# Cosine attention and a gelu MLP: a new order of the opening and the second batch, and scalings shared by two engines

## The chip, the cores and the metric

The kernel runs on one core of a Trainium2 chip. The metric is device time in microseconds of one execution, as the median of several runs; less is better. One further execution, recorded by the hardware profiler, gives the trace that all stage times come from.

## The reference

The computation is attention with normalised queries and keys, followed by a two-layer MLP with the exact gelu. In short:

```python
# q, k, v: [8, 12, 448, 64] float32, tau = 0.1
q_n = q / (norm(q, axis=-1) + 1e-6)
k_n = k / (norm(k, axis=-1) + 1e-6)
attn = softmax((q_n @ k_n.T) / tau)
o = attn @ v
x = o.transpose(0, 2, 1, 3).reshape(3584, 768)   # heads side by side
h = x @ w_in                                     # 768 x 2048
y = gelu_exact(h) @ w_out                        # 2048 x 768, float32
```

## The kernel before, in words

**Tiling.** Four heads of a batch are a *quad*: three quads per batch, 24 in all, numbered 0 to 23. A quad's sequence of 448 is cut into 7 chunks of 64 rows per head. The very first quad is worked in two halves of two heads, so the kernel counts *units*: units 0 and 1 are the halves of quad 0, unit 2 is quad 1, unit 3 is quad 2, and so on. Tiles of loaded data carry the quad's number (`qk0`, `sq0_0` for the squares of Q, `sq0_1` for those of K, `qkb0` for the scaled bf16 copy, `qkT0` for its transpose); the tiles around a norm (`nq`, `rn`) carry the number of a *group* of units whose roots are taken together.

**The steps of a quad.** `load_qk` (L127) loads Q and K with DMAs that SyncE issues (the first K by ScalarE), into a pool of four buffers. `square` (L173 on ScalarE, L175 on another engine) squares them, `reduce` (L183, VectorE) sums over the 64 elements of a row. `logs` and `roots` (ScalarE, L190 and L195) take the square root as exp(0.5 ln), into a tile `root2` or `root4` that has the 1e-6 beside each root; `inverses` (L201 and L203, VectorE) adds it and takes the reciprocal `rn`. `scale` (L219) multiplies Q and K with `rn` and writes bf16: 448 columns for a half of quad 0, 896 for Q or K of a whole quad. `transposes` turns the result, either on TensorE (L236, into a PSUM tile `tp` that `copies`, L241, brings back to SBUF on VectorE) or by a DMA (L231, issued by SyncE). `scores` (L257) multiplies K and Q of two chunks into one pair of PSUM banks, `exps` (L267, ScalarE) takes the exponential into bf16. The row sums come from `sums` (TensorE) or from folded additions of VectorE (`gather`) or GpSimd, `turned`, `inverted` and `spread` (VectorE) make their reciprocals, `values` (L346, TensorE) multiplies with v, and `normalise` (L380, VectorE) writes the batch's `x_t`, bf16.

**The MLP.** For one batch `mm` (L493, called the *hp* passes) accumulates 16 tiles of 128 columns of w_in over six slices of 128 rows (`kd`), 96 passes per batch; `gelu` (L522, L1357) evicts each. Two batches share one `g`. The second matmul (L427, the *op* passes) runs in *pieces* of 16 passes (one per `kf`, four small matmuls each); the last pass of a piece evicts it with a VectorE reduction (L436), or with a ScalarE copy and a VectorE addition (L434) where the caller asks for that. `run(n)` issues the next n passes from the list that `output_pieces` makes. Batch 0 has six pieces in that list, of three tiles by two halves of the columns.

**What sets the order.** Nothing schedules automatically: each engine executes its instructions in the order in which the Python code issues them, and waits by semaphores for what others have to deliver. For the first three batches this order is written out by hand in `opening()` (L538), a list of some 500 calls in which the attention of quads 0 to 2, the hp passes of batch 0, the attention of quads 3 to 5 with op passes between, and the start of batch 1's MLP are interleaved. Later batches follow rules in `attention` and `first`.

**Queues.** SyncE issues the loads of q and k, the transposing DMAs and the stores, in order. GpSimd issues the loads of v, of w_in (`load_wi`, L467: parts 0 and 1 hold kd 0 to 3 for all columns, parts 2 and 3 hold kd 4 and 5 for half of the columns each; two DMAs a part) and of w_out (`load_wo`, L473, four parts), all between its arithmetic. `late_copy` (L1371) is a copy of one column on GpSimd that waits for quad 0's last data; it stands ahead of GpSimd's first load. `spin` (L489) issues matmuls whose result nobody uses. `behind` and `rest_v` hold back the rest of batch 1's v until an exponential is done.

Of the kernel before, what the change touches and what calls it, by code (L numbers as in the profile page):

```python
# [16 lines left out]
def kernel(  # L17
# [17 lines left out]
    nc = tc.nc  # L35
# [444 lines left out]
    def upto(f, n, last=None):  # L480
        last = {load_qk: NG, load_v: NV, root: len(groups), load_wi: NQ + 1, load_wo: 4}.get(f, NU)
# [56 lines left out]
    def opening():  # L538
        load_qk(0)
        table(EXP_SET)  # L540
        load_qk(1)
        load_qk(2)
        spin(20)
        late_copy()
        load_qk(3)
        x_t[0] = xp.tile([128, KD, S], BF16, tag="x", name="x0")
        square(0, ((AC, Q),))
        square(0, ((AC, K),))
        reduce(0, Q)
# [44 lines left out]
        spin(2)
        scores(0, ((0, 4), (0, 5)))
        scale(2, ((GP, 0),))
        reduce(3, Q)
        exps(0, ((0, 4), (0, 5)))
        spin(1)
        scores(0, ((1, 0), (1, 1)))  # L600
        reduce(3, K)
        exps(0, ((1, 0), (1, 1)))
        spin(1)
        scores(0, ((1, 2), (1, 3)))
        scale(2, ((GP, 1),))
        load_qk(5)
        transposes(2, 0)
        exps(0, ((1, 2), (1, 3)))
        sums(0, (0,))
        copies(2, 0)  # L610
        scores(0, ((1, 4), (1, 5)))
        logs(3)
        scores(0, ((0, 6), (1, 6)))
        roots(3)
        transposes(2, 1)
        exps(0, ((1, 4), (1, 5)))
        inverses(3)
        sums(0, (1,))
        scale(3, ((GP, 0),))
        copies(2, 1)  # L620
        sums(0, (2,))
        exps(0, ((0, 6), (1, 6)))
        sums(0, (3,))
        sums(0, (4,))
        scores(1, ((0, 0), (1, 0)))
        scores(1, ((0, 1), (1, 1)))
        sums(0, (5,))
        exps(1, ((0, 0), (1, 0)))
        sums(0, (6,))
# [24 lines left out]
        exps(1, ((0, 4), (1, 4)))
        sums(1, (1,))
        scores(1, ((0, 5), (1, 5)))
        normalise(0, 0)
        transposes(3, 1)
        exps(1, ((0, 5), (1, 5)))
        scores(1, ((0, 6), (1, 6)))  # L660
        copies(3, 1)
        sums(1, (2,))
        square(4, ((GP, Q),))
        square(5, ((GP, Q),))
        square(5, ((GP, K),))
        load_wo(0)
        load_wo(1)
        exps(1, ((0, 6), (1, 6)))
# [767 lines left out]
```

## Time and profile before

| | us |
|---|---|
| median of three runs | 391.37 (391.14 to 391.41) |
| span of the profiled execution | 390.6 |
| TensorE busy in it | 382.6 (98%) |
| VectorE busy | 273.0 (70%) |
| ScalarE busy | 269.9 (69%) |
| GpSimd busy | 248.7 (64%) |
| mean granted TensorE clock | 1.000 of full speed |

The span runs from the first to the last instruction of the profiled execution; the runs' time of that execution is not recorded, and the median of the runs lies 0.8 above the span. Engines are PE (TensorE matmuls), PEld (its weight loads), DVE (VectorE), ACT (ScalarE), POOL (GpSimd) and SP (SyncE). In rows of groups stand the line and engine, the operation, the tile written and the tiles read, the count, and then busy time, mean nanoseconds of one and the idle time before with what ended most of it. In rows of a timeline stand the start, the length, the engine and the operation. A row of busy times by stretch has the stretch, its length, then the busy microseconds and counts of PE, PEld, DVE, ACT and POOL, the granted clock, the DMA share and the rate in GB/s. Line numbers are those of the kernel before.

### The profile page before, as it was taken

Reading aid. Unit: us, or ns where it says so; the run is one execution under the profiler, and the core shown is the slowest. Engines: PE = TensorE matmul, PEld = TensorE weight load, DVE = VectorE, ACT = ScalarE, POOL = GpSimd, SP = SyncE. Lnnn points to the kernel's source line nnn. Section 1 sums busy time; section 2 is a strip of 40 time slices with the busy share of each in tenths; the row PEclk is TensorE's granted clock in tenths of the full one; section 3 lists DMA queues with packets and bytes.
Section 4 is the critical chain, followed back from the end, with each engine's and each line's share of the span. In section 5 each row is a group of like instructions: output and inputs, shape, how many; then the busy total and the mean of one; then the engine's idle time right before and its main releaser. Section 6 shows DMA issues by size and latency. Waiting matters only on the chain.

```text
span 390.6 us, 13166 instructions
## 1 busy us (share of the span) xinstructions
PE 382.6 (98%) x5820; PEld 236.6 (61%) x5820; DVE 273.0 (70%) x509; ACT 269.9 (69%) x391; POOL 248.7 (64%) x161
## 2 busy tenths in 40 slices
PE   7899999999999999999999999999999999999996
PEld 3444568555777656865567556775567555655674
DVE  4878439876778896879696896889685993670032
ACT  5895789857999958996678767997577646504300
POOL 4796950557998399969594794969595770910000
PEclk9999999999999999999999999999999999999999
DMA  8999999926899691889067490876045600130033
GB/s 265 264 262 229 176 191 329 254 56 157 179 203 299 112 217 69 185 158 275 5 172 130 120 243 2 185 131 118 3 91 81 154 9 2 44 82 2 7 79 83
DMA packets 64473, 54.85 MB, mean 140 GB/s; under 512 B 38688, under 2 KB 60320, under 8 KB 64416
## 3 DMA queue, kind: packets, MB, share of 16 engines
q1 hardware_dynamic: 54464, 41.79, 42.0%
q0 software_dynamic: 9568, 11.80, 18.5%
q8 instruction: 45, 0.74, 0.8%
q10 hardware_dynamic: 384, 0.43, 0.4%
q14 instruction: 12, 0.10, 0.1%
HBM read 45.61 MB, written 11.01 MB: 145 GB/s over the span
## 4 chain that ended last, share of the span: by engine, by line
PE 95%; DMA 2%; SPq 1%; ACT 1%; issue 0%; DVE 0%; ACTq 0%
PE hp L493 37%; PE op L427 36%; PE st L257 9%; PE o L346 8%; DMA qk<-in_k_dram 2%; PE op L451 1%; PE sm L323 1%; PE sm L332 1%; PE tp L236 1%; SPq L134 1%; ACT sq L173 0%; ACT pt L267 0%; PE spin L489 0%; DVE last L454 0%; ACT root L195 0%
## 5 line engine op out<-in xcount | busy, mean ns | idle before, releaser
L427 PE MATMUL op<-wo,g 64*64 64x384 bf16 x3456 | 167.1, 323 | 0.2 <-issue 0.2
L267 ACT ACTIVATE pt<-st 128x896 bf16<-128x896 f32 x168 | 147.2, 918 | 19.6 <-PE st L257 17.5
L493 PE MATMUL hp<-x,wi 128*128 128x448 bf16 x768 | 147.0, 353 | 0.0
L427 PEld LDWEIGHTS <-g 64*64 64x64 bf16 x3456 | 106.2, 107 | 40.9 <-issue 4.2
L493 PEld LDWEIGHTS <-wi 128*128 128x128 bf16 x768 | 74.3, 98 | 71.6 <-issue 3.2
L219 POOL TENSOR_TENSOR qkb<-qk,rn 128x896 bf16<-128x896 f32 (+1 forms) x49 | 80.4, 1662 | 46.0 <-DVE rn L203 37.9
L278 POOL TENSOR_TENSOR acc<-acc,pt 128x896 f32<-128x896 f32 x55 | 103.8, 1888 | 4.3
L436 DVE TENSOR_REDUCE ot<-op 128x384 f32<-128x768 f32 x50 | 47.3, 946 | 54.7 <-PE op L427 47.5
L1357 ACT ACTIVATE g<-hp 128x448 bf16<-128x448 f32 x96 | 46.2, 547 | 55.1 <-PE hp L493 55.1
L257 PE MATMUL st<-qkT 64*64 64x448 bf16 x672 | 62.8, 352 | 0.5 <-ACT pt L267 0.5
L183 DVE TENSOR_REDUCE nq<-sq 128x14 f32<-128x896 f32 (+1 forms) x50 | 50.4, 1036 | 13.6 <-ACT sq L173 7.1
L380 DVE TENSOR_TENSOR x<-o,rs 128x448 bf16<-128x448 f32 x48 | 27.6, 611 | 22.9 <-PE o L346 21.9
L175 POOL TENSOR_TENSOR sq<-qk 128x896 f32<-128x896 f32 x16 | 26.6, 1685 | 23.8 <-DMA qk<-in_q_dram 13.3
L346 PE MATMUL o<-pt,v 64*64 64x448 bf16 x672 | 39.5, 349 | 0.0
L290 DVE TENSOR_TENSOR acc<-acc,pt 128x896 f32<-128x896 f32 x30 | 33.0, 1099 | 1.0
L173 ACT ACTIVATE sq<-qk 128x896 f32<-128x896 f32 (+1 forms) x33 | 28.8, 901 | 4.4 <-DMA qk<-in_q_dram 3.2
L257 PEld LDWEIGHTS <-qkT 64*64 64x64 bf16 x672 | 23.1, 106 | 11.7 <-issue 3.7
L375 DVE STREAM_TRANSPOSE rs<-rc 128x448 f32<-128x448 f32 x48 | 28.1, 621 | 0.4
L278 POOL TENSOR_TENSOR acc<-pt 128x896 f32<-128x896 bf16 x11 | 20.7, 1878 | 10.9 <-ACT pt L267 10.9
L346 PEld LDWEIGHTS <-v 64*64 64x64 bf16 x672 | 21.1, 107 | 9.2 <-issue 0.2
L522 ACT ACTIVATE g<-hp 128x448 bf16<-128x448 f32 x32 | 15.4, 547 | 12.8 <-PE hp L493 12.7
L295 DVE TRANSPOSE_TENSOR_REDUCE sa<-acc 128x28 f32<-128x896 f32 x17 | 18.8, 1104 | 0.2
(54 smaller groups left out, 176.0 us busy)
## 6 DMA issues: line engine op xcount, KB each, us to landing
qk<-in_q_dram SPq DMA_DIRECT2D x23, 448.0 KB, 4.9
qk<-in_k_dram SPq DMA_DIRECT2D x23, 448.0 KB, 5.8
out_dram<-ot SPq DMA_DIRECT2D x48, 192.0 KB, 4.0
v<-in_v_dram POOLq DMA_DIRECT2D x6, 672.0 KB, 7.2
wo<-in_moe_w_out_dram POOLq DMA_DIRECT2D x4, 768.0 KB, 10.6
wi<-in_moe_w_in_dram POOLq DMA_DIRECT2D x4, 512.0 KB, 13.8
out_dram<-ot SPq DMA_DIRECT2D x12, 96.0 KB, 2.1
wi<-in_moe_w_in_dram POOLq DMA_DIRECT2D x4, 256.0 KB, 14.1
```

What stands on the lines that cost most here:

```text
L173: eng.activation(sq, t, AF.Square)
L183: nc.vector.tensor_reduce(nq_t[n][:, j, i], sq_t[g, i][:, s0:s1], mybir.AxisListType.X, ALU.add)
L219: eng.tensor_tensor(qkb[:, i, :, s0:s1].rearrange("p c s d -> p s c d"), t[:, i, s0:s1], rn[:, i].to_broadcast([128, s1 - s0, C, D]), ALU. ...
L257: nc.tensor.matmul(st[cols, n, :S], lhsT=qkT[rows, 1, c, cols], rhs=qkT[rows, 0, :, cols], start=True, stop=True, tile_position=(64 * s, 6 ...
L267: nc.scalar.activation(pt, st[:, :, :S], AF.Exp, scale=inv_tau)
L278: nc.gpsimd.tensor_tensor(acc_t[g], all_t[g][:, 0] if c == 1 else acc_t[g], all_t[g][:, c], ALU.add)
L290: nc.vector.tensor_tensor(acc_t[g], acc_t[g], all_t[g][:, c], ALU.add)
L346: nc.tensor.matmul(bank_t[g, h][cols, :S], lhsT=v_t[g][rows, s, c, :], rhs=pt_t[g, s, c][rows], start=(c == 0), stop=(c == C - 1), tile_po ...
L427: nc.tensor.matmul(ps[cols, r, :NH], lhsT=g_t[sb][rows, kf, t * 128 + 64 * c:t * 128 + 64 * (c + 1)], rhs=wo[rows, kf, ni * NH:(ni + 1) * NH],
L436: nc.vector.tensor_reduce(part, ps[:, :, :NH].rearrange("p r d -> p d r"), mybir.AxisListType.X, ALU.add)
L493: nc.tensor.matmul(t, lhsT=wi[:, kd, m * 128:(m + 1) * 128], rhs=x_t[b][:, kd, :], start=(kd == 0), stop=(kd == KD - 1))
L1357: nc.scalar.activation(g_t[sb][:, m, hf * S:(hf + 1) * S], hps.pop(m), AF.Gelu)
```

## The change

- **A new order in `opening()`.** Nearly all of its calls stand in another place. Unit 1's squares, reduces and roots are interleaved with unit 0's as before, but VectorE's copies of quad 0's transposes now precede quad 1's reduces, and on ScalarE the first exponentials precede the squares of quad 2. Both `load_v` of the first batch stand ahead of `load_wi(0)`. In the second batch the scores and exponentials of quads 3, 5 and 4 are interleaved with op passes in another sequence, with quad 5's first scores ahead of quad 4's.
- **Scalings and squares shared.** VectorE takes the scalings of K for quad 0's first half, of Q for quad 1, of K for quad 2, and of Q and K for quads 4 and 5; GpSimd had them all, and keeps the rest. GpSimd takes the square of Q for quad 0's second half and that of K for quad 2, which ScalarE had.
- **Buffers of the loads.** `gate(3)` allocates quad 3's tile early and lets GpSimd set two elements of each partition to zero in it; quad 3's load writes the same tile and so stands behind that. `late_copy`, which reads quad 0's tile, is moved into the second batch, so that this buffer stays in use until then; quads 4 and 5 take the buffers of quads 1 and 2, where they took those of quads 0 and 1.
- **Own root for quad 5.** Group 5 now holds quad 4 alone, and quad 5 is a new group 19 (`NR`) with its own tile `root6`; its logs and roots are called beside group 5's.
- **Output pieces of batch 0.** The first two pieces are interleaved: 12 passes of the first, 12 of the second, then the last 4 of each.
- `spin`: 20 + 8 passes become 20 + 2. `attend(g, c, p)` is written as its two calls in the later batches, which changes nothing there.

```diff
+    root2 += [consts.tile([128, 4 * C, 2], F32, name=f"root6_{n}") for n in range(1)]
...
+    groups[NQ + 2] = [NQ + 2]
+    NR = len(groups)
+    groups.append([NQ + 3])
...
-        t = qkp.tile([128, 2, 2, C, D], F32, tag="qk", name=f"qk{g}")
+        t = qk_t[g] if g in qk_t else qkp.tile([128, 2, 2, C, D], F32, tag="qk", name=f"qk{g}")
...
+    def gate(g):
+        qk_t[g] = qkp.tile([128, 2, 2, C, D], F32, tag="qk", name=f"qk{g}")
+        nc.gpsimd.memset(qk_t[g][:, :, 0, 0, 0:1], 0.0)
...
-        sr_t[n] = root2[2 if len(groups[n]) == 2 else n % 2][:, :math.prod(shapes[n])]
+        sr_t[n] = root2[3 if n == NR else 2 if len(groups[n]) == 2 else n % 2][:, :math.prod(shapes[n])]
...
     def opening():
...
+        scale(0, ((GP, Q),))
...
+        scale(0, ((DV, K),))
...
-        fill = [f for t, ni in todo if t not in tail for f in second_pieces(sb, t, ni)]
+        pieces = [second_pieces(sb, t, ni) for t, ni in todo if t not in tail]
+        if b == 0:
+            n = KF * 3 // 4
+            one, two = pieces[:2]
+            pieces[:2] = [one[:n] + two[:n] + one[n:] + two[n:]]
+        fill = [f for p in pieces for f in p]

Three places show how instructions move. The first is GpSimd's opening, from its first work on quad 0 to the scalings of quad 1. In the kernel before (`qkb` is the scaled copy, `rn0` and `rn1` are the reciprocals of quad 0's halves, `v0` and `v1` the loads of v, `wi` those of w_in):

```order
L1371 COPY late_166<-qk0_133 128x1
L155 DMA v0_180<-in_v_dram 128x2x448
L467 DMA wi_131<-in_moe_w_in_dram 64x2x2048 x2
L219 TENSOR_TENSOR qkb0_197<-qk0_133,rn0_192 128x7x64 x2
L219 TENSOR_TENSOR qkb0_197<-qk0_133,rn1_221 128x7x64 x2
L155 DMA v1_260<-in_v_dram 128x4x448
L467 DMA wi_131<-in_moe_w_in_dram 64x2x2048 x2
L219 TENSOR_TENSOR qkb1_297<-qk1_139,rn2_285 128x2x7x64 x2
L219 TENSOR_TENSOR qkb2_364<-qk2_142,rn3_360 128x2x7x64
```

And in the changed kernel, from the same point:

```order
L183 TENSOR_TENSOR sq0_0_141<-qk0_135 128x448
L145 MEMSET qk3_155 128x2
L163 DMA v1_157<-in_v_dram 128x4x448
L227 TENSOR_TENSOR qkb0_165<-qk0_135,rn0_163 128x7x64
L163 DMA v0_230<-in_v_dram 128x2x448
L227 TENSOR_TENSOR qkb0_165<-qk0_135,rn1_209 128x7x64 x2
L475 DMA wi_133<-in_moe_w_in_dram 64x2x2048 x2
L183 TENSOR_TENSOR sq2_1_287<-qk2_227 128x896
L227 TENSOR_TENSOR qkb1_307<-qk1_151,rn2_302 128x2x7x64
```

One scaling with `rn0` instead of two is left on GpSimd, `v1` is loaded ahead of `v0` and of that scaling, and the first `wi` loads have moved from ahead of quad 0's scalings to behind them. A square stands at the start and another ahead of quad 1's scaling, of which GpSimd keeps one half.

The second place is VectorE's opening, from the reduces of quad 0's first half. Before (`nq` are the sums of squares, `se` and `rn` the inverses, `tp` the PSUM tiles of the transposes, `qkT0` quad 0's transposed copy):

```order
L183 TENSOR_REDUCE nq0_176<-sq0_0_172 128x7
L183 TENSOR_REDUCE nq0_176<-sq0_1_174 128x7
L183 TENSOR_REDUCE nq1_184<-sq0_0_172 128x7
L201 TENSOR_REDUCE se0_190<-root2_0_125 128x14
L203 RECIPROCAL rn0_192<-se0_190 128x14
L183 TENSOR_REDUCE nq1_184<-sq0_1_174 128x7
L183 TENSOR_REDUCE nq2_201<-sq1_0_194 128x14
L201 TENSOR_REDUCE se1_219<-root2_1_126 128x14
L203 RECIPROCAL rn1_221<-se1_219 128x14
L241 COPY qkT0_208<-tp0_1_209 64x896
L241 COPY qkT0_208<-tp0_0_225 64x896
```

And changed:

```order
L191 TENSOR_REDUCE nq0_143<-sq0_0_141 128x7
L191 TENSOR_REDUCE nq0_143<-sq0_1_145 128x7
L191 TENSOR_REDUCE nq1_159<-sq0_0_141 128x7
L209 TENSOR_REDUCE se0_161<-root2_0_125 128x14
L211 RECIPROCAL rn0_163<-se0_161 128x14
L191 TENSOR_REDUCE nq1_159<-sq0_1_145 128x7
L227 TENSOR_TENSOR qkb0_165<-qk0_135,rn0_163 128x7x64
L209 TENSOR_REDUCE se1_207<-root2_1_126 128x14
L211 RECIPROCAL rn1_209<-se1_207 128x14
L249 COPY qkT0_198<-tp0_0_199 64x896
L249 COPY qkT0_198<-tp0_1_212 64x896
L191 TENSOR_REDUCE nq2_234<-sq1_0_174 128x14
```

VectorE now scales one part of `qkb0` itself, right behind the reduce of the second half, and the first two copies to `qkT0` stand ahead of the reduces of quad 1 (`nq2`), of which one stood ahead of them.

The third place is GpSimd's work behind quad 2's scaling (`qkb2`), where the last parts of w_in are loaded. Before:

```order
L219 TENSOR_TENSOR qkb2_364<-qk2_142,rn3_360 128x2x7x64
L467 DMA wi_131<-in_moe_w_in_dram 64x2x1024 x2
L219 TENSOR_TENSOR qkb2_364<-qk2_142,rn3_360 128x2x7x64
L467 DMA wi_131<-in_moe_w_in_dram 64x2x1024 x2
L175 TENSOR_TENSOR sq3_1_464<-qk3_168 128x896
L175 TENSOR_TENSOR sq3_0_492<-qk3_168 128x896
L175 TENSOR_TENSOR sq4_0_494<-qk4_241 128x896
```

And changed:

```order
L227 TENSOR_TENSOR qkb2_365<-qk2_227,rn3_363 128x2x7x64
L183 TENSOR_TENSOR sq3_1_430<-qk3_155 128x896
L475 DMA wi_133<-in_moe_w_in_dram 64x2x1024 x2
L183 TENSOR_TENSOR sq3_0_439<-qk3_155 128x896
L183 TENSOR_TENSOR sq4_0_449<-qk4_275 128x896
L475 DMA wi_133<-in_moe_w_in_dram 64x2x1024 x2
L481 DMA wo_134<-in_moe_w_out_dram 128x4x768 x2
```

The square of quad 4's Q (`sq4_0`) has moved from behind the last `wi` loads and quad 3's squares to ahead of the last `wi` loads; one of the two scalings of quad 2 is no longer here (VectorE has it).

More of the change, by code (lines that the diff above doesn't have):

```diff
@@ L612, in opening @@
-        logs(3)
-        scores(0, ((0, 6), (1, 6)))
+        exps(0, ((0, 0), (0, 1)))
+        square(3, ((GP, K),))
+        scores(0, ((0, 4), (0, 5)))
+        exps(0, ((0, 4), (0, 5)))
+        scores(0, ((1, 0), (1, 1)))
+        inverses(2)
+        exps(0, ((1, 0), (1, 1)))
+        reduce(3, Q)
+        scale(2, ((GP, K),))
+        scores(0, ((1, 2), (1, 3)))
+        exps(0, ((1, 2), (1, 3)))
+        more(0)
+        reduce(3, K)
+        scores(0, ((0, 6), (1, 6)))
+        transposes(2, 1)
@@ L663, in opening @@
[L663 to L668, printed above, removed]
+        bank(0, 13)
+        load_wo(2)
+        sums(1, (0,))
+        sums(1, (1,))
+        exps(1, ((0, 4), (1, 4)))
+        sums(1, (2,))
+        spread(0, 0)
+        copies(3, 0)
+        normalise(0, 0)
+        scores(2, ((0, 0), (1, 0)))
+        values(1, (0,))
+        values(1, (1,))
+        scores(2, ((0, 2), (1, 2)))
@@ L803, in opening @@
+        mm(0, 9, 0, 6)
+        gelu(0, 7)
+        gelu(0, 14)
+        run(1)
+        run(1)
+        run(1)
+        gelu(0, 6)
+        run(1)
+        run(1)
+        run(1)
+        run(1)
+        run(1)
+        inverses(5)
+        inverses(19)
+        copies(4, 1)
+        scale(6, ((DV, K),))
+        gelu(0, 9)
+        scores(3, ((0, 0), (1, 0)), 0)
         run(1)
@@ L805, in opening @@
         run(1)
-        gelu(0, 9)
-        scale(5, ((GP, Q),))
+        run(1)
+        scale(6, ((DV, Q),))
+        run(1)
+        run(1)
+        table(EXP_SET)
+        exps(3, ((0, 0), (1, 0)))
+        scores(3, ((0, 1), (1, 1)), 1)
+        run(1)
+        exps(3, ((0, 1), (1, 1)))
+        scale(5, ((DV, K),))
+        scale(5, ((DV, Q),))
+        behind(3, 1)
+        late_copy()
+        load_v(2)
+        rest_v()
+        run(1)
+        scores(3, ((0, 4), (1, 4)), 0)
+        exps(3, ((0, 4), (1, 4)))
@@ L808, in opening @@
+        run(1)
+        run(1)
+        run(1)
+        run(1)
+        run(1)
+        run(1)
+        run(1)
+        run(1)
+        transposes(6)
+        scores(3, ((0, 3), (1, 3)), 1)
+        run(1)
+        gather(3, 1)
+        scores(3, ((0, 2), (1, 2)), 0)
+        exps(3, ((0, 3), (1, 3)))
+        exps(3, ((0, 2), (1, 2)))
         transposes(5)
         run(1)
-        gelu(0, 13)
-        table(EXP_SET)
-        run(3)
-        scores(3, ((0, 0), (1, 0)), 0)
-        scores(3, ((0, 1), (1, 1)), 1)
@@ L833, in opening @@
+        run(1)
+        run(1)
+        run(1)
+        run(1, AC)
+        scores(5, ((0, 1), (1, 1)), 1)
+        scores(5, ((0, 6), (1, 6)), 0)
+        exps(5, ((0, 1), (1, 1)))
         gather(3, 2)
         gather(3, 3)
-        run(5)
-        attend(3, 4, 0)
+        gather(3, 4)
+        run(1)
+        run(1)
+        run(1)
+        run(1)
+        run(1)
+        run(1)
+        run(1)
+        run(1)
+        load_qk(9)
+        banks(1, 4, 3)
+        load_qk(7)
+        load_qk(6)
@@ new lines, in opening @@
+        load_qk(8)
+        exps(5, ((0, 6), (1, 6)))
+        scores(4, ((0, 6), (1, 6)), 1)
+        run(1)
+        run(1)
+        run(1)
+        square(7, ((GP, Q),))
+        square(8, ((GP, Q),))
+        scores(5, ((0, 2), (1, 2)), 0)
+        square(7, ((GP, K),))
+        square(9, ((GP, Q),))
+        square(8, ((GP, K),))
+        square(9, ((GP, K),))
+        run(1)
+        run(1)
+        run(1)
+        exps(4, ((0, 6), (1, 6)))
+        run(1)
+        load_v(3)
+        exps(5, ((0, 2), (1, 2)))
```

538 lines of the change are left out of this document (251 added, 287 removed).

## The prediction

> **What bounds the kernel now.** I read the page first, then busy times by stage, then the chain of waits in order of time, then the timelines of the opening. The page's busy row and the row of the chain that ended last:
>
> ```profile
> PE 382.6 (98%) x5820; PEld 236.6 (61%) x5820; DVE 273.0 (70%) x509; ACT 269.9 (69%) x391; POOL 248.7 (64%) x161
> PE 95%; DMA 2%; SPq 1%; ACT 1%; issue 0%; DVE 0%; ACTq 0%
> ```
>
> TensorE is busy 382.6 of 390.6 us and holds 95% of the chain. The change adds and removes no matmul except six spins (28 before, 22 after), so it can only move TensorE's idle time. Busy time by stage (columns: stretch, its length, then each engine's busy us; PEclk is the granted clock):
>
> ```profile
> 8.00:14.00 6.00, 4.37 (x41) 2.26 (x41) 4.04 (x8) 4.46 (x9) 4.86 (x6) 1.00 1.12 321
> 14.00:20.00 6.00, 5.48 (x52) 2.33 (x51) 4.92 (x9) 5.97 (x10) 4.60 (x5) 1.00 1.06 248
> 20.00:33.30 13.30, 13.29 (x189) 6.19 (x190) 10.63 (x18) 12.12 (x15) 13.28 (x12) 1.00 1.10 257
> 33.30:52.00 18.70, 18.70 (x116) 9.93 (x116) 8.64 (x16) 12.01 (x22) 15.54 (x11) 1.00 1.09 194
> 52.00:77.70 25.70, 25.70 (x586) 17.85 (x585) 20.16 (x39) 22.26 (x29) 7.71 (x6) 1.00 1.12 265
> ```
>
> A busy TensorE is not TensorE at work: between 14 and 20 us it is 5.48 busy with 52 matmuls of small tiles, three of them spins. There ScalarE is the full engine, 5.97 of 6.00. From 33.3 us on TensorE is full and useful. Three rows of the chain mark the borders:
>
> ```profile
> 3.70 8.88 DMA qk<-in_k_dram
> 12.66 0.95 ACT sq L173
> 33.35 13.35 PE hp L493 x70
> ```
>
> Up to 33.35 us TensorE waits for the first batch's attention; what comes after is work that no reordering shortens. So the gain is how much earlier than 33.35 the hp run starts, less every wait that the new order adds behind it. Any TensorE wait behind that point costs its full length.
>
> **The opening, step by step.** VectorE, GpSimd and TensorE around quad 0's first half (start, us, engine):
>
> ```profile
> 7.14 0.24 DVE L203 RECIPROCAL rn<-se 128x14 f32<-128x14 f32 x1
> 7.38 0.62 DVE L183 TENSOR_REDUCE nq<-sq 128x7 f32<-128x448 f32 x1
> 10.70 1.08 DVE L241 COPY qkT<-tp 64x896 bf16<-64x896 bf16 x2
> 5.77 0.89 POOL L155 DMA_DIRECT2D v<-in_v_dram  x1
> 6.65 1.22 POOL L467 DMA_DIRECT2D wi<-in_moe_w_in_dram  x2
> 7.86 1.86 POOL L219 TENSOR_TENSOR qkb<-qk,rn 128x448 bf16<-128x448 f32 x2
> 12.36 0.57 PE L257 MATMUL st<-qkT 64*64 64x448 bf16 x4
> ```
>
> The prices of the moved operations:
>
> ```profile
> L219 POOL TENSOR_TENSOR qkb<-qk,rn 128x448 bf16<-128x448 f32 x4 | 3.7, 951 | 1.1 <-DVE rn L203 1.1
> L219 DVE TENSOR_TENSOR qkb<-qk,rn 128x896 bf16<-128x896 f32 x1 | 1.1, 1092 | 0.0
> ```
>
> The reciprocal rn ends at 7.38. Now GpSimd is still issuing v and wi until 7.86, then scales K and Q one after the other until 9.72. After, GpSimd issues only v ahead of it and scales Q from about 7.45 to 8.4; VectorE scales K behind its reduce that ends at 8.00. That is 0.6 (half of 1.09, rounded up), or until 9.0 if it must wait for GpSimd (below). I take 9.0. The K transposes then end near 9.6, the second inverse (0.4) runs meanwhile, the two copies (1.08) end near 10.45, and the first scores start at 10.5 instead of 12.36. The old copies stood behind a reduce of quad 1 on VectorE; that reduce now stands behind them.
>
> GpSimd also takes a square of 448 (0.95 at most, by its scaling row) and one of 896 that ScalarE did. ScalarE is where the time then goes:
>
> ```profile
> 13.99 4.13 ACT L267 ACTIVATE pt<-st 128x896 bf16<-128x896 f32 x5
> 20.35 10.29 ACT L267 ACTIVATE pt<-st 128x896 bf16<-128x896 f32 x12 [0.16 <-PE st L257]
> 27.20 5.21 ACT L267 ACTIVATE pt<-st 128x896 bf16<-128x896 f32 x6
> 12.66 0.95 ACT L173 ACTIVATE sq<-qk 128x896 f32<-128x896 f32 x1 [0.97 <-DMA qk<-in_k_dram]
> ```
>
> Now the first exp starts at 13.99, because the squares of three quads come first and wait for their data (0.97 in the last row), and the 21st ends at 32.41 (27.20 + 5.21). After: exp 1 from 11.1 to 12.0; a square (0.95), a log and a root (0.55, with overlap) to 13.3; four exps at 0.80 (13.99 and 4.13 for five) to 16.5; log, exp, root, exp to 18.6; a wait of 0.3 for quad 1's copies; 14 exps at 0.86 (10.29 / 12) from 18.9 to 30.9. That is 1.5 earlier. The tail from the 21st exp to the hp run was 0.94 (33.35 - 32.41) and stays, so the hp run starts near 31.8: **gain 1.55**. With exps at 0.80 throughout it is 2.4; with the K scaling, the copies and the waits each 0.4 worse it is 0.4.
>
> The six spins removed cost nothing: the granted clock is 1.00 in every row above, also where TensorE is busy 4.37 of 6, and TensorE's longest pause in the new order is about a microsecond.
>
> **GpSimd beside VectorE.** One place shows both engines scaling at once:
>
> ```profile
> 87.84 1.09 DVE L219 TENSOR_TENSOR qkb<-qk,rn 128x896 bf16<-128x896 f32 x1
> 90.33 1.10 DVE L175 TENSOR_TENSOR sq<-qk 128x896 f32<-128x896 f32 x1
> 87.89 6.74 POOL L219 TENSOR_TENSOR qkb<-qk,rn 128x896 bf16<-128x896 f32 x3 [0.38 <-DVE rn L203]
> 14.84 3.33 POOL L219 TENSOR_TENSOR qkb<-qk,rn 128x896 bf16<-128x896 f32 x2 [0.19 <-DVE rn L203]
> ```
>
> Undisturbed, GpSimd needs 3.33 for two (1.67 each). Beside two VectorE operations on two SBUF inputs, three take 6.74 instead of 5.0, while VectorE keeps 1.09 and 1.10. So GpSimd lost 1.7 us, nearly all of the overlap, where VectorE started first by 0.05. In the new order quad 2's scaling is such a pair: the K half follows its own reciprocal on VectorE, so it should start first, near 18.9 by the sequence above, and GpSimd's Q half ends near 21.7 instead of 20.6. Its transposes on TensorE come near 21.8, after the copies of K: price about 0. The Trainium skill, "SBUF — State Buffer", section "SBUF: two separate sides", says that the pair of ports is an exclusive lock, taken by whichever starts first for its whole instruction. These rows agree for VectorE first; none shows GpSimd first, where by that rule VectorE would wait.
>
> **Loads.** Now q3 is issued at once, and q4 and q5 as soon as quads 0 and 1 have been scaled. After, q3 waits for GpSimd's memset (about 6.2), q4 for both scalings of quad 1 (about 17.2) and q5 for those of quad 2 (about 21). The wi loads start later, 11.4 instead of 6.65, behind both v loads. Traffic per queue at 19 to 23 us (v under way), then at 25 to 29 (wi); then the issue of the last wi pair, the landing times of all wi loads, and those of q4 and q5:
>
> ```profile
> q0 software_dynamic: 424, 0.38, 57.2%
> q1 hardware_dynamic: 422, 0.72, 55.6%
> q0 software_dynamic: 182, 0.68, 83.8%
> q1 hardware_dynamic: 181, 0.30, 23.1%
> 23.91 1.26 POOL L467 DMA_DIRECT2D wi<-in_moe_w_in_dram  x2
> DMA to landing us min/median/max: 10.0/14.1/17.3
> qk<-in_q_dram SPq DMA_DIRECT2D x1, 448.0 KB, 10.9
> qk<-in_q_dram SPq DMA_DIRECT2D x1, 448.0 KB, 15.9
> ```
>
> The two queues send packet for packet (424 to 422, 182 to 181), so q0 moves 0.095 MB/us of v and 0.17 of wi whatever q1 has. From about 10 us: both v (0.69 MB) to 17.3, wi's first 2.1 MB to 29.6, the last 1.05 MB to about 36.5: last landing near 37.5, like now (23.9 and 14.1 make 38.0 for the pair). The last wi piece is needed 38 hp passes into the run, at 0.190 each (row below): 31.8 + 7.2 = 39.0. Cover: 1.5 us, against 2 now. If the cover goes, TensorE waits for the difference.
>
> **Second batch.** Quads 4 and 5 are now scaled on VectorE, behind the second PE transpose of quad 3, and their transposing DMAs are used sooner (quad 5's scores come before quad 4's). For the two now, and for 96 hp and 96 op passes:
>
> ```profile
> L231 SPq DMA_TRANSPOSE qkT<-qkb x2: 2170/2468/2767, 51.9 to 54.2; - x2
> DMA to landing us min/median/max: 5.5/5.9/6.3
> 77.76 18.27 PE hp L493 x96
> 365.89 15.72 PE op L427 x384
> ```
>
> From that PE transpose: 0.5, copy 0.6, two scalings 2.2, landing 5.5 to 6.3: 8.8 to 9.6. TensorE gets there after 0.5 + 12 hp passes (2.3) + 32 op passes of 0.164 (5.2) + 5 scores of 0.19 (1.0) = 9.0. So quad 5 is late by 0 to 0.6. Quad 4's follows two scalings later (11.0 to 11.8), needed at 10.6: late by 0.4 to 1.2, the first delay included. I take 0.4, the end for the least traffic, since wo is nearly loaded then. The rest here (evictions first in the interleaved pieces, exps between) keeps covers of 0.1 to 0.5 by the same counting; I take 0 and keep 0.5 as the bound. The own root for quad 5 and the extra table load lie under the hp run, where ScalarE is 12.01 busy of 18.70. The two long pieces of tail and all later batches are untouched.
>
> **The sum.** 390.6 - 1.55 + 0.4 = 389.45 for the span, a gain of 1.15. The median of the runs, 391.37, stands 0.8 above the profiled span; I keep that: 390.2.
>
> **Rivals.**
> 1. *Given back in the second batch* (0.18): transposes at their late end (1.2) and a late eviction or exp (0.5) eat the gain: 391.5. For it: TensorE is full there, so every wait counts. Against: traffic is lower than where the 6.3 landing was seen.
> 2. *GpSimd first on the shared ports* (0.10): at quad 2, VectorE's K scaling waits out GpSimd's 1.67; TensorE's transposes, copies and ScalarE's exps shift by about 1.2, and 391.4 results. Against: in both pairs of the rows VectorE started first. This is what the skill's lock would make of the pair.
> 3. *The last wi load behind quad 4* (0.14, slower): in GpSimd's row a square on q4 now stands ahead of the last wi loads. If q4, issued at 17.2, lands after 10.9 to 15.9 like q4 and q5 now, it is there at 28.1 to 33.1, wi is issued 1.7 to 2.3 later, and with the shortest landing of its rows, 10.0, comes at 40 to 45 instead of 37.5. From 41 on (39.0 + 1.15 + 0.8) the kernel is slower; at 43 TensorE waits 4: 394.2. Against: q1 is shorter then, so q4 should land near 26.
>
> **How the numbers follow.** The measurement tells 0.2% (0.8 us) from no change. The forecast, 389.1 to 390.6, has 0.58 and is faster by more than that; rivals 1 and 2 lie within it (0.28); rival 3 is slower (0.14). The low end is a gain of 2.4 with nothing given back: 389.0. The upper end takes in rivals 1 and 2 and a wi load one microsecond late beyond its cover and the gain: 392.1.
>
> **What would show it.** In the profile after: first scores near 10.5, first exp near 11.1, 21st exp ending near 30.9, the hp run starting near 31.8, no TensorE idle until 56; wi landing before 39; quad 5's first scores with at most half a microsecond of wait. A hp run that starts after 32.6, or waits of over 1 us behind it, would make the forecast wrong.

## The result, and the profile after

| | before | after |
|---|---|---|
| median of the runs | 391.38 (14 runs, 390.36 to 393.22) | 393.64 (14 runs, 392.21 to 396.39) |
| profiled execution: span | 390.6 | 391.6 |
| hp run of batch 0 starts | 33.29 | 32.41 |
| first op pass | 51.95 | 51.17 |
| hp run of batch 1 starts | 77.69 | 78.02 |
| first op pass behind it | 95.95 | 97.01 |

The changed kernel is slower: ratio 1.0054, 95% interval 1.0037 to 1.0071. A gain of 1.2 was forecast; the time lies 2.3 above the kernel before, and above the upper end of 392.1. Each run also has a mean granted TensorE clock, and it matters here: 7 of the 14 runs of the changed kernel lie below 0.998, and below I call the others *full-clock runs* (median 392.44) and compare like with like.

The page of the changed kernel, its busy row and the chain that ended last:

```profile
PE 382.6 (98%) x5814; PEld 236.1 (60%) x5814; DVE 279.8 (71%) x519; ACT 270.9 (69%) x393; POOL 240.6 (61%) x157
PE 83%; DMA 5%; issue 4%; POOL 3%; DVE 2%; ACT 1%; SPq 1%; POOLq 0%
```

TensorE is as busy as before, but the chain now leaves it for 17% of the span instead of 5%: loads of q, squares and VectorE's work stand in it. Busy times in the stretches that were shown of before:

```profile
14.00:20.00 6.00, 5.51 (x46) 2.18 (x45) 5.42 (x8) 4.40 (x8) 3.62 (x4) 0.72 1.13 214
52.00:77.70 25.70, 24.97 (x568) 18.35 (x560) 20.95 (x39) 21.63 (x27) 7.63 (x7) 1.00 0.91 239
```

Two things are new. From 14 to 20 us the granted clock is 0.72, where it was 1.00, and ScalarE, which was full there, is busy 4.40 of 6. And between 52 and 77.7 us TensorE, which had been full, lacks 0.73. Microsecond by microsecond the clock drop looks like this (columns as before, the clock is the third number from the end):

```profile
15.00:16.00 1.00, 0.81 (x11) 0.50 (x10) 1.00 (x2) 1.00 (x3) 1.00 (x2) 1.00 1.23 223
16.00:17.00 1.00, 1.00 (x9) 0.42 (x8) 0.97 (x2) 1.00 (x4) 0.65 (x2) 0.62 1.11 225
17.00:18.00 1.00, 1.00 (x11) 0.61 (x10) 0.60 (x2) 0.89 (x2) 0.00 (x0) 0.50 1.05 209
19.00:20.00 1.00, 1.00 (x12) 0.23 (x10) 0.92 (x1) 0.52 (x1) 0.97 (x1) 0.67 1.03 209
```

The opening, in the timelines of TensorE and ScalarE:

```profile
9.89 0.56 PE L265 MATMUL st<-qkT 64*64 64x448 bf16 x4 [0.79 <-DVE qkT L249]
10.50 0.92 ACT L275 ACTIVATE pt<-st 128x896 bf16<-128x896 f32 x1 [0.64 <-PE st L265]
19.48 11.15 ACT L275 ACTIVATE pt<-st 128x896 bf16<-128x896 f32 x13 [1.60 <-PE st L265]
32.41 8.97 PE L501 MATMUL hp<-x,wi 128*128 128x448 bf16 x46
```

The first scores and the first exponential come even earlier than forecast (10.5 and 11.1), but under the half clock ScalarE waits 1.60 for scores, and of the 1.93 that e10 below has at full clock only 0.88 is left when the hp run starts. Behind it, up to 110 us, TensorE's timeline shows three waits:

```profile
71.52 0.84 PE L435 MATMUL op<-wo,g 64*64 64x384 bf16 x16 [0.59 <-DVE x L388]
82.55 14.54 PE L501 MATMUL hp<-x,wi 128*128 128x448 bf16 x76 [0.57 <-DVE x L388]
104.10 1.17 PE L435 MATMUL op<-wo,g 64*64 64x384 bf16 x24 [0.54 <-DVE ot L444]
```

From the first op pass to the next hp run the kernel before takes 25.74, the changed one 26.85; the hp run itself takes 0.73 more from its first to its last pass (18.71 against 17.98); from there to the hp run of the third batch it takes 0.24 more (34.47 against 34.23). With 0.78 gained up to the first op pass, 1.11 + 0.73 + 0.24 - 0.78 makes 1.3 lost, and what follows gives 0.2 back: the spans differ by 1.1. (Every run's time is 1.8 above its span, so that the profiled execution of before, 390.6, was a run of about 392.4 and not one at the median; the forecast's 0.8 was wrong by this.)

### The profile page after: what moved, and what is told of

It is laid out like the page before. It is cut to its first block, busy times and chain, and to the rows that moved or that the text cites. A ratio compares the mean times of both kernels' runs of the same rounds, so it can differ in the third digit from the quotient of the medians.

```text
span 391.6 us, 13173 instructions
## 1 busy us (share of the span) xinstructions
PE 382.6 (98%) x5814; PEld 236.1 (60%) x5814; DVE 279.8 (71%) x519; ACT 270.9 (69%) x393; POOL 240.6 (61%) x157
## 4 chain that ended last, share of the span: by engine, by line
PE 83%; DMA 5%; issue 4%; POOL 3%; DVE 2%; ACT 1%; SPq 1%; POOLq 0%
PE hp L501 33%; PE op L435 31%; PE st L265 8%; PE o L354 7%; DMA qk<-in_q_dram 5%; POOL sq L183 2%; PE op L459 1%; PE sm L331 1%; ACT pt L275 1%; PE tp L244 1%; SPq L138 1%; SPq L239 1%; DVE nq L191 1%; POOL qkb L227 1%; PE sm L340 0%
## 5 line engine op out<-in xcount | busy, mean ns | idle before, releaser
L435 PE MATMUL op<-wo,g 64*64 64x384 bf16 x3456 | 165.9, 323 | 1.1 <-DVE x L388 0.6
L275 ACT ACTIVATE pt<-st 128x896 bf16<-128x896 f32 x168 | 147.1, 919 | 20.8 <-PE st L265 18.8
L501 PE MATMUL hp<-x,wi 128*128 128x448 bf16 x768 | 147.5, 353 | 0.6 <-DVE x L388 0.6
L435 PEld LDWEIGHTS <-g 64*64 64x64 bf16 x3456 | 105.5, 107 | 41.3 <-issue 3.8
L501 PEld LDWEIGHTS <-wi 128*128 128x128 bf16 x768 | 74.2, 98 | 72.3 <-issue 4.2
L227 POOL TENSOR_TENSOR qkb<-qk,rn 128x896 bf16<-128x896 f32 (+1 forms) x42 | 69.7, 1677 | 48.7 <-DVE rn L211 41.8
L444 DVE TENSOR_REDUCE ot<-op 128x384 f32<-128x768 f32 x50 | 47.2, 945 | 47.7 <-PE op L435 47.6
L265 PE MATMUL st<-qkT 64*64 64x448 bf16 x672 | 63.4, 355 | 1.5 <-DVE qkT L249 0.8
L191 DVE TENSOR_REDUCE nq<-sq 128x14 f32<-128x896 f32 (+1 forms) x50 | 50.4, 1036 | 11.5 <-POOL sq L183 6.2
L183 POOL TENSOR_TENSOR sq<-qk 128x896 f32<-128x896 f32 (+1 forms) x18 | 29.3, 1640 | 29.4 <-DMA qk<-in_q_dram 20.5
L388 DVE TENSOR_TENSOR x<-o,rs 128x448 bf16<-128x448 f32 x48 | 27.6, 611 | 22.9 <-PE o L354 22.4
L265 PEld LDWEIGHTS <-qkT 64*64 64x64 bf16 x672 | 22.8, 107 | 14.0 <-issue 4.3
L181 ACT ACTIVATE sq<-qk 128x896 f32<-128x896 f32 (+1 forms) x31 | 27.3, 910 | 1.9 <-DMA qk<-in_q_dram 1.7
L530 ACT ACTIVATE g<-hp 128x448 bf16<-128x448 f32 x32 | 15.6, 544 | 12.5 <-PE hp L501 12.4
```

The source lines that it names most:

```text
L183: eng.tensor_tensor(sq, t, t, ALU.mult)
L191: nc.vector.tensor_reduce(nq_t[n][:, j, i], sq_t[g, i][:, s0:s1], mybir.AxisListType.X, ALU.add)
L227: eng.tensor_tensor(qkb[:, i, :, s0:s1].rearrange("p c s d -> p s c d"), t[:, i, s0:s1], rn[:, i].to_broadcast([128, s1 - s0, C, D]), ALU. ...
L265: nc.tensor.matmul(st[cols, n, :S], lhsT=qkT[rows, 1, c, cols], rhs=qkT[rows, 0, :, cols], start=True, stop=True, tile_position=(64 * s, 6 ...
L275: nc.scalar.activation(pt, st[:, :, :S], AF.Exp, scale=inv_tau)
L435: nc.tensor.matmul(ps[cols, r, :NH], lhsT=g_t[sb][rows, kf, t * 128 + 64 * c:t * 128 + 64 * (c + 1)], rhs=wo[rows, kf, ni * NH:(ni + 1) * NH],
```

## The experiments

Each kernel ran up to twelve times, beside runs of the kernel before on the same chip. *Full* counts runs with a mean clock of 0.998 or more, and gives their median; *stretch* is the time from the first op pass to the next hp run in the profiled execution, *run* from there to that run's last pass.

| kernel | median | full | before, full, same chip | stretch | run |
|---|---|---|---|---|---|
| e1 more spins | 393.29 | 7 of 7: 393.29 | 391.30 | 26.86 | 18.71 |
| e2 new opening only | 392.35 | 3 of 12: 390.44 | 391.30 | 25.97 | 17.98 |
| e3 new second batch only | 399.71 | 2 of 6: 395.3 | 391.30 | 26.85 | 18.71 |
| e4 before without spins | 394.67 | 2 of 12: 391.2 | 391.30 | 25.74 | 17.98 |
| e5 sums first | 392.98 | 12 of 12: 392.98 | 391.82 | 26.66 | 17.98 |
| e6 v load early | 393.34 | 12 of 12: 393.34 | 391.82 | 26.85 | 18.72 |
| e7 pieces in turn | 394.80 | 7 of 7: 394.80 | 391.82 | 26.82 | 18.71 |
| e8 new opening, ten spins | 392.09 | 11 of 12: 392.0 | 391.82 | 26.96 | 17.98 |
| e9 gather early | 394.22 | 12 of 12: 394.22 | 391.63 | 27.59 | 18.72 |
| e10 new opening, four spins | 390.81 | 12 of 12: 390.81 | 391.63 | 25.74 | 17.98 |
| e11 as e10, GpSimd scales | 392.10 | 12 of 12: 392.10 | 391.63 | 25.74 | 17.98 |
| e12 mended | 391.57 | 11 of 12: 391.47 | 391.63 | 26.70 | 17.98 |
| e13 mended, quad 3 first | 391.08 | 12 of 12: 391.08 | 391.76 | 26.13 | 17.98 |
| e14 as e10, VectorE scales 4 and 5 | 391.91 | 11 of 12: 391.89 | 391.76 | 26.27 | 17.98 |

Full-clock runs of one kernel still scatter, from lowest to highest, by 1.3 to 4.2 us, so a few tenths are read from the traces and not from the medians. One of e8's twelve runs took 1418 us at a clock of 1.000, why is not known; *full* leaves it out. The theories: A, the clock falls because the spins are gone; B, the new second batch makes TensorE wait for VectorE; C, the last w_in load is late (rival 3).

**e1, more spins.**

```diff
         transposes(0, 1)
+        spin(2)
...
-        spin(1)
+        spin(2)
...
         scores(0, ((0, 4), (0, 5)))
+        spin(2)
```

The middle edit stands twice and the last one also behind the next two scores.

> The changed kernel with ten more spin passes between 9 and 16 us, where TensorE waits. Theory A (the clock): the half clock at 16.4 to 19.8 us is gone, the mean granted clock is 1.000 in every run, the hp run starts near 31.3 instead of 32.4, and the time falls by 1.0 to 1.5 to about 392.3. Theory B (the waits for VectorE in the second batch, at 71 and 82 us, hold the end): the hp run may start earlier but these waits absorb or keep it; time 393.0 to 393.6. If spins were free to leave out, clock and time stay as they are (393.6).

The clock stayed at 1.000 (lowest run 0.999), so the first half of A holds. The time did not come down as A had it: the hp run starts at 31.89, not 31.3. ScalarE's timeline shows why; four exponentials took 3.33 in the changed kernel and take longer behind doubled spins:

```profile
12.73 3.87 ACT L275 ACTIVATE pt<-st 128x896 bf16<-128x896 f32 x4
31.89 4.44 PE L501 MATMUL hp<-x,wi 128*128 128x448 bf16 x22
```

And the waits behind the hp run are all there (stretch 26.86, run 18.71): 2.0 above the kernel before at the same full clock, as B expected.

**e2 and e3, each half of the change alone.** e2 has the changed list up to the first hp run and from there the order of before, GpSimd scaling quads 4 and 5, and these parts undone; e3 has the old list up to the hp run and all that is changed behind it. Both, and the kernels made from e2, also hold a table that says which of two PSUM buffers some tiles take.

```diff
-    groups[NQ + 2] = [NQ + 2]
-    groups.append([NQ + 3])
...
-            pieces[:2] = [one[:n] + two[:n] + one[n:] + two[n:]]
```

> The new order up to the first hp run, then the old order, the old joint root of quads 4 and 5, GpSimd scaling them, and output pieces one after the other. Theory B (the loss lies in the second batch): the gain of the opening (0.9 in the profile) stands alone, time 390.5 against 391.4 of the kernel before. Theory A (the loss is the half clock): the dip is still there in most runs and the time stays at or above 391.4. Theory C (the last w_in load is late): hp passes wait at 38 to 41 us and the time is above 392.

> The old order up to the first hp run, with its 28 spins, then the changed kernel's order, scalings, own root and interleaved pieces. Theory B: waits of 0.5 to 0.6 at about 72 and 83 us, time 1.5 to 1.9 above the kernel before, 393.0 to 393.3. Theory A or C: no loss here, 391.4, and a granted clock of 1.000.

In e2 the second batch takes its old time again (25.97 and 17.98), and its three full-clock runs lie 0.9 under those of before: B's number. In the other nine the clock falls, and the median is 392.35: A's number. Both are true at once. In e3 the new second batch has the same 26.85 and 18.71 behind an old opening, so this loss belongs to the second half. e3's time is far above B's, though: in its trace the squares wait 1.68 and 2.03 for loads in the opening, the clock is at half for 6.8 us, and the hp run starts at 37.84. The clock falls in four of its six runs, and the other two still lie 4.0 above before; why the old opening fared so badly there is open.

**e4, the kernel before without its eight spins behind the first twenty.**

```diff
-        spin(2)
-        spin(1)
...
```

> The kernel before without its eight spins behind the first twenty. Theory A: the granted clock falls to half for one window of 3.4 us or more in most runs (mean 0.996 or less), and the time rises by 0.5 to 1.7, to about 392.4. If leaving out spins is free, as the prediction had it: 391.4 and a mean clock of 1.000.

A, and stronger than expected: ten of twelve runs lose clock (7 of before's 24 on that chip do) and the median of all runs rises by 3.0 (ratio of the compared runs 1.0064, interval 1.0035 to 1.0094), while the two full-clock runs stand level with before. The granted clock in its trace:

```profile
16.00:17.00 1.00, 1.00 (x9) 0.65 (x9) 0.59 (x2) 1.00 (x3) 1.00 (x1) 0.52 1.09 248
17.00:20.00 3.00, 3.00 (x21) 1.38 (x21) 1.53 (x4) 2.15 (x4) 2.01 (x3) 0.50 1.08 258
20.00:22.00 2.00, 2.00 (x16) 0.50 (x14) 0.08 (x1) 0.38 (x1) 2.00 (x3) 0.50 1.15 280
```

Half clock lasts here from 16 to about 22.9 us, twice the 3.4 us of the changed kernel.

**e5, quad 5's row sums first** (on e1).

```diff
+        sums(5, p=0)
         values(5, (0,), p=2)
...
-        sums(5, p=0)
```

> The changed kernel with the ten more spins (which held the clock) and, in the second batch, quad 5's row sums ahead of its product with v instead of behind it. Theory B1 (the hp run at 82 us waits for the normalising of quad 5 because its sums come last on TensorE): the gap of 0.57 behind twenty hp passes is gone, and the time is 0.5 to 0.7 below the kernel with the spins alone, 392.5 against 393.2. If VectorE is simply full there, the gap stays.

The gap in the hp run is gone, one piece of 96 passes as before:

```profile
77.86 18.33 PE L501 MATMUL hp<-x,wi 128*128 128x448 bf16 x96
```

B1 is shown. The sums had come last on TensorE, and VectorE's chain from them to quad 5's x (4.4 us, from 78.1 to 82.5 in the changed kernel, its first and last row below) ended after the twentieth hp pass, which was the last that could do without it. The time is 1.2 above before on its chip, where e1 lay 2.0 above on its own, which fits the expected fall, though a few tenths are within the scatter.

```profile
78.14 0.65 DVE L362 STREAM_TRANSPOSE tr<-sm 128x448 f32<-128x448 f32 x1 [1.38 <-PE sm L340]
81.38 1.12 DVE L388 TENSOR_TENSOR x<-o,rs 128x448 bf16<-128x448 f32 x2
```

**e6, the load of v for batch 2 early** (on e1).

```diff
         square(8, ((GP, Q),))
+        load_v(3)
...
-        load_v(3)
```

> The changed kernel with the ten more spins, and the load of v for batch 2 issued by GpSimd behind two squares, as in the kernel before, instead of behind six. Theory B3 (that load goes out at 88 us instead of 73 us and lies beside the transposing DMAs and the loads of q and k from 91 to 99 us, so that a square, a reduce and an eviction come late and the op passes wait 0.5 at about 103 us): the wait is gone, 392.7 against 393.2. If the wait comes from the later start of everything by one microsecond, it stays.

GpSimd's timeline, of e1 and of e6:

```profile
87.96 0.89 POOL L163 DMA_DIRECT2D v<-in_v_dram  x1
97.95 3.32 POOL L183 TENSOR_TENSOR sq<-qk 128x896 f32<-128x896 f32 x2 [2.77 <-DMA qk<-in_q_dram]
```

```profile
73.01 0.89 POOL L163 DMA_DIRECT2D v<-in_v_dram  x1
96.82 3.32 POOL L183 TENSOR_TENSOR sq<-qk 128x896 f32<-128x896 f32 x2 [1.45 <-DMA qk<-in_q_dram]
```

With the load back at 73 us the squares that wait for quad 10's load start 1.1 earlier, and the wait for VectorE's eviction near 103 us is gone: the third cause is shown. (That wait stands in every trace with the late load, 0.26 to 1.35, and in none with the early one.) The median did not fall (393.34); a few tenths are below what its runs, from 392.38 to 396.41, can tell.

**e7, output pieces in turn** (on e1).

```diff
-            pieces[:2] = [one[:n] + two[:n] + one[n:] + two[n:]]
```

> The changed kernel with the ten more spins, and the first two output pieces one after the other, as before, instead of interleaved. Theory B2 (the waits of 0.6 to 0.8 at 70 us and 0.3 at 75 us come from the order of evictions on VectorE ahead of quad 3's normalising): the first wait shrinks by half or more, 392.6 against 393.2. If they come from the order in which the exponentials of quads 3, 5 and 4 are mixed, interleaving changes nothing: 393.0 to 393.4, or the waits move to about 56 us.

The wait stays and the stretch is 26.82, so interleaving is not its cause. The time is 3.0 above before, where e1's was 2.0; its trace waits 0.98 near 104 us instead of 0.26, and why is open.

```profile
71.14 0.84 PE L435 MATMUL op<-wo,g 64*64 64x384 bf16 x16 [0.50 <-DVE x L388]
```

**e8, new opening with ten spins, old second batch** (e2 with e1's spins).

> The new opening with ten more spins and the old second batch. Theories A and B together: every run has a clock of 1.000, the hp run starts near 31.9, the second batch takes its old 25.7 to 26.0 us from the first op pass to the next hp run, and the time is 390.0 to 390.4, under the 391.3 of the undisturbed runs of the kernel before. If the spins cost time in the opening, it is 390.7 or more.

The clock holds, but the time is level with before (ratio 0.9994, interval 0.9974 to 1.0013). Its first hp passes start 0.7 later than with fewer spins (30.39 against 29.68 in e10 below), and this trace also loses time in the stretch (26.96) to stops that no wait explains (last section).

**e9, one of quad 3's additions early** (on e1).

```diff
         gather(3, 1)
+        gather(3, 4)
```

> The changed kernel with the ten more spins, and one of quad 3's six additions on VectorE (chunk 4) put ahead of the eviction for which VectorE idles 1.04 us at 56 us. Theory B2' (quad 3's normalising is late because evictions that are not ready stand ahead of its additions on VectorE): the additions, and so the end of quad 3's normalising, come about 1 us earlier, the gap of 0.6 to 0.8 before the op passes at 70 us is gone or under 0.2, the one of 0.3 at 75 us too, and the stretch from the first op pass to the next hp run falls from 26.85 to 25.8 to 26.2. If the exponentials are what comes late, the additions wait for them and the gap stays.

B2' fell. VectorE does the addition earlier and then idles 1.05 at the next eviction; the additions end at 64.7, no earlier than in e1 (64.5), and quad 3's normalising at 71.9 (71.0):

```profile
61.63 0.56 DVE L442 TENSOR_TENSOR ot<-ot,op 128x384 f32<-128x384 f32 x1 [1.05 <-ACT ot L441]
62.45 2.29 DVE L291 TENSOR_TENSOR acc<-acc,pt 128x896 f32<-128x896 f32 x2 [0.27 <-ACT pt L275]
```

The second row has the clue: the last two additions wait for exponentials. (The gap at 70 us is gone in this trace only because TensorE itself had lost 0.98 just before, see the last section; the time is 2.6 above before, more than e1's 2.0.)

**e10, new opening with four single spins, old second batch.**

```diff
         transposes(0, 1)
+        spin(1)
         scores(0, ((0, 4), (0, 5)))
+        spin(1)
```

The last edit stands behind the next two scores too.

> The new opening with four more spin passes (26 in all instead of 32 or 22) and the old second batch. Theory A with a dose: four single passes already keep the clock at 1.000 in most runs and delay no scores, so that the time is 0.5 to 1.0 under the undisturbed runs of the kernel before. If the clock still falls in most runs, the number of passes decides, and the time is that of the kernel without them (392.3 on the first chip).

```profile
31.36 13.41 PE L501 MATMUL hp<-x,wi 128*128 128x448 bf16 x70
75.77 18.33 PE L501 MATMUL hp<-x,wi 128*128 128x448 bf16 x96
```

Four passes are enough: no run of twelve lost clock, the hp run starts 1.93 earlier than in the trace of before, and the full-clock median is 0.8 under before (ratio of all compared runs 0.9978, interval 0.9953 to 1.0002, so this gain is not clear of no change). The two traces differ by more than the medians, 2.1 against 0.8, because e10's profiled run lies 0.6 below its median and that of before some 0.7 above the median here.

What the four passes do to TensorE shows in the 3.4 us ahead of the place where the clock fell; before, the changed kernel and e10:

```profile
12.80:16.20 3.40, 2.88 (x24) 1.15 (x22) 2.55 (x5) 3.37 (x6) 3.21 (x4) 1.00 1.05 244
12.80:16.20 3.40, 2.71 (x26) 1.25 (x27) 3.27 (x6) 3.40 (x6) 3.29 (x4) 1.00 1.24 238
12.80:16.20 3.40, 3.40 (x29) 1.27 (x30) 3.27 (x6) 3.40 (x7) 3.29 (x4) 1.00 1.23 234
```

TensorE is busy 2.71 of 3.40 in the changed kernel, and 3.23 or more in every trace with four or ten spins added. In e4 it was 2.29 and in e3 1.77 in the 3.4 us before the fall.

**e11, the same with all opening scalings on GpSimd.**

```diff
-        scale(0, ((DV, K),))
+        scale(0, ((GP, K),))
...
```

> As the kernel with the new opening and four more spins, but GpSimd does all scalings of quads 0, 1 and 2. Theory D (the shared scalings are what brings the scores forward): the first scores come 0.4 to 0.5 later, quad 1's and quad 2's transposes up to 1 us, and the hp run starts 0.5 to 1.0 later. If the gain of the opening comes from the order alone, the start stays within 0.2.

```profile
14.07 3.33 POOL L227 TENSOR_TENSOR qkb<-qk,rn 128x896 bf16<-128x896 f32 x2
19.35 3.33 POOL L227 TENSOR_TENSOR qkb<-qk,rn 128x896 bf16<-128x896 f32 x2 [0.76 <-PE st L265]
```

The hp run starts at 32.66, 1.30 later, and the time is 1.3 higher: D holds, and more than half of the opening's gain is the sharing. It comes from quads 1 and 2 (the rows); the first scores start at 10.00, no later than e10's 10.02.

**e12, mended:** the changed kernel with e10's four spins, e5's, e6's and e9's edits.

> The changed kernel with four more spins, quad 5's sums first, the load of v early and one addition early. All theories together: no TensorE wait over 0.2 at 70, 75, 82 and 103 us, a clock of 1.000 in most runs, and 1.5 to 2.5 below the changed kernel on the same chip, about level with the kernel before or up to 1.0 under it. If the removed waits only make others due, it stays above the kernel before.

The waits at 75, 82 and 104 us are gone, the one at 70 us is not (0.38 in the row); the full-clock median is 391.47, 1.0 under the changed kernel's (on another chip) and level with before.

```profile
71.16 0.84 PE L435 MATMUL op<-wo,g 64*64 64x384 bf16 x16 [0.38 <-DVE x L388]
```

**e13, mended, and quad 3's last exponentials first.**

```diff
-        scores(5, ((0, 1), (1, 1)), 1)
-        scores(5, ((0, 6), (1, 6)), 0)
+        scores(3, ((0, 5), (1, 5)), 1)
+        scores(3, ((0, 6), (1, 6)), 0)
...
```

> The mended kernel with quad 3's last two scores, exponentials and additions ahead of quad 5's first two instead of behind them. Theory B4 (quad 3's normalising is late because its last exponentials come late, behind those of quads 5 and 4): the additions end 2 us earlier, the wait of 0.6 at 70 us is gone, the stretch from the first op pass to the next hp run falls from 26.7 to 25.8 to 26.1, and the time is 0.5 to 0.9 below the mended kernel, 390.6 to 391.0 where the kernel before has 391.6. If VectorE is simply full from 57 to 71 us, or quad 5 and 4 then come late instead, the stretch stays at 26.5 or more.

```profile
57.64 4.61 DVE L291 TENSOR_TENSOR acc<-acc,pt 128x896 f32<-128x896 f32 x4
68.73 1.11 DVE L388 TENSOR_TENSOR x<-o,rs 128x448 bf16<-128x448 f32 x2
76.24 18.33 PE L501 MATMUL hp<-x,wi 128*128 128x448 bf16 x96
```

B4 is shown: the four remaining additions run without a pause, normalising ends at 69.8, and no TensorE wait over 0.2 is left between 34 and 123 us. The stretch is still 0.39 longer than the old 25.74, at the same number of matmuls and with no wait in a row; where this goes is open. The full-clock median is 0.7 under before; ratio of all compared runs 0.9947, interval 0.9914 to 0.9979, part of which is that four of before's 23 runs lost clock and e13's did not. It is a version that beats both kernels, but not e10, which keeps the old second batch (0.8 under before).

**e14, e10 with VectorE scaling quads 4 and 5.**

```diff
-        scale(6, ((GP, K),))
+        scale(6, ((DV, K),))
...
```

> The new opening with four more spins and the old second batch, whose scalings of quads 4 and 5 VectorE does instead of GpSimd. If these scalings are what filled VectorE in the second batch: waits of 0.3 or more appear between 52 and 82 us and the time is 0.5 or more above the kernel with GpSimd scaling them. If, as the trace has it, VectorE is idle at that place (46 to 54 us): the stretch from the first op pass to the next hp run stays within 0.2 of 25.74 and the time within 0.4.

Half a miss. TensorE waits for VectorE nowhere from 52 to 82 us, so these scalings do not fill VectorE there. The stretch is 26.27 all the same; its two longest stops, op matmuls at 66.2 and 72.4 us that start 0.38 and 0.43 behind the one ahead, have no wait that the profile names (last section). The time is 1.1 above e10's (on another chip), and this trace loses 1.68 earlier, where gelus stand behind the common root of quads 4 and 5, whose squares had waited for loads. That is not the edit's doing, as the first moved scaling starts at 45.24, behind that root:

```profile
46.71 0.94 PE L244 MATMUL tp<-ident,qkb 128*128 128x128 bf16 x14 [1.68 <-ACT g L530]
```

## Why the prediction was wrong

- **"The six spins removed cost nothing" failed.** It took a granted clock of 1.00 with TensorE at 4.37 of 6, and pauses of at most a microsecond, as enough. The changed kernel is at 4.75 of 6 from 8 to 14 us, its longest wait there is 0.79, and the clock still halves for 3.4 us. The price is 1.05 of the hp run's start (32.41 against e10's 31.36); e4 shows the same loss in the kernel before (3.0 in the median, ten of twelve runs), e10 the cure (four passes, no run of twelve). The busy share of one stretch does not foretell it: before had 2.88 of 3.40 ahead of that place and kept its clock in the trace, yet lost it in some other runs. What rule it follows is open. The Trainium skill, "TensorE: Matmul & The Clock Gate", section "Part 1: The HAM clock gate", has the half clock as the state after a window of 3.4 us in which TensorE idles. The levels (0.50 and 1.00) and the length (3.4 here, 6.8 in e4) agree with these traces; that condition does not, since TensorE is busy 2.71 of the 3.40 us ahead of the drop.
- **The rest of the opening was right.** Forecast: hp run at 31.8, a gain of 1.55 with a high end of 2.4. At full clock, with four spins more than the change has, it is 31.36 (e10), 1.93; in the changed kernel the half clock leaves 32.41. The medians bear out only 0.8 of it (see e10). The sharing on which it rests is worth 1.3 (e11).
- **"The rest here ... I take 0 and keep 0.5 as the bound" failed by the most.** Behind the first op pass the changed kernel loses 2.1 (1.11 + 0.73 + 0.24), where the sum had 0.4. Three orders were not followed to their waits: quad 5's sums behind its product with v (0.73 in the run, e5), quad 3's last exponentials behind those of quads 5 and 4 (e13 takes 0.57 of e12's stretch away, and 0.72 of the changed kernel's), and the load of v. The other 0.39 of the stretch is not explained.
- **"All later batches are untouched" was wrong** by the load of v, which the new order put behind four more squares in GpSimd's queue (e6). Behind the third hp run they were: from there to the end the traces of before and after take 260.7 and 260.4.
- **The 0.4 for the transposing DMAs was too much.** They land after 3.6 to 5.3 instead of 5.5 to 6.3, and no score waits more than 0.2 for them. The two in the second batch:

```profile
L239 SPq DMA_TRANSPOSE qkT<-qkb x2: 1476/1528/1579, 51.7 to 53.7; - x2
DMA to landing us min/median/max: 3.6/4.4/5.3
```

- **Rival 1** named the place, the second batch, and nearly the size (1.7 against 1.11 + 0.73), but its larger part was the transposing DMAs, which cost nothing, so that the size is luck. **Rival 3** had the sign, but not by its mechanism: GpSimd's square waits for quad 4 as described (1.88, until 27.89, between the 26 and the 28.1 to 33.1 that were forecast), yet the w_in loads land after 7.4 to 12.5 and no hp pass waits.

```profile
27.89 1.68 POOL L183 TENSOR_TENSOR sq<-qk 128x896 f32<-128x896 f32 x1 [1.88 <-DMA qk<-in_q_dram]
DMA to landing us min/median/max: 7.4/8.3/12.5
```

- **The shared ports behaved as forecast.** At quad 2 VectorE starts first, keeps 1.09, and GpSimd takes 2.44 instead of 1.67. At quad 0 GpSimd starts first, which no row of before had shown:

```profile
7.06 0.93 POOL L227 TENSOR_TENSOR qkb<-qk,rn 128x448 bf16<-128x448 f32 x1 [0.42 <-DVE rn L211]
7.51 0.96 DVE L227 TENSOR_TENSOR qkb<-qk,rn 128x448 bf16<-128x448 f32 x1
18.83 1.09 DVE L227 TENSOR_TENSOR qkb<-qk,rn 128x896 bf16<-128x896 f32 x1
19.03 2.44 POOL L227 TENSOR_TENSOR qkb<-qk,rn 128x896 bf16<-128x896 f32 x1 [2.38 <-DVE rn L211]
```

VectorE's scaling of 448 columns ends at 8.47, 0.48 after GpSimd's at 7.99; half of its 1.09 for 896 columns is 0.55. So it waited the other out, as the lock that the prediction quotes from the Trainium skill would have it. Rival 2's place did not occur.

What stays open: at full clock the changed kernel is 0.6 to 1.1 above before, by the chip; the other 1.2 between the two medians is the clock, by the runs' own records. The traces' 1.1 does not check this, as the changed kernel's trace has the half clock in it and that of before is a run above its median. Why the profiled execution of before was a microsecond above its median is not shown, as it is the only trace of that kernel; nor is where the 0.39 go that e13's stretch keeps, or what makes the clock fall in one run and not in the next.

## What to carry to other kernels

Matmuls that only keep TensorE busy are part of the schedule: when an order is changed, count them anew, look at the granted clock of many runs and not of one profile, and use as few as hold it, since with ten the hp run started 0.7 later than with four. When TensorE is full, an order that brings one quad forward sets another back: follow each moved row to the buffer it frees, on every queue, down to a load that slips behind four squares. A gain of an opening is easily worked out from durations; the losses behind it came from positions in queues.

## What the runs showed of the hardware that was not expected

The clock halves in whole pieces of about 3.4 us (3.41 in the changed kernel and e2, 6.83 in e3 and e4) without any long pause of TensorE (the longest from 8 us to the fall is 0.79 in the changed kernel and 1.62 in e3), and differently from run to run: the kernel before, with its 28 spins, also lost clock in 22 of its 112 runs beside the experiments, down to a mean of 0.981 and up to 399.1 us. And TensorE sometimes stops where nothing in the profile holds it, mostly near 65 and 125 us and twice near 72, for 0.1 to 1.0 us, and in some traces not at all; in e2 and in e9:

```profile
125.93 0.81 PE L435 MATMUL op<-wo,g 64*64 64x384 bf16 x13 [0.70 <-issue]
```

```profile
66.08 1.00 PE L435 MATMUL op<-wo,g 64*64 64x384 bf16 x19 [0.98 <-issue]
```

In one trace they add up to at most 1.6 us (e8), so they can make up part of the scatter among full-clock runs; their cause was not tried.
